# Attention and mixture of experts on one core: widest block first, register reads moved, fills placed anew

## The chip, the cores and the metric

The kernel runs on one core of a Trainium2 chip. The metric is the time of one execution on the device in microseconds (us). Beside timed runs there is one execution under the hardware profiler, with a trace of every engine: TensorE (PE, and PEld for its loads of weights), VectorE (DVE), ScalarE (ACT), GpSimd (POOL) and SyncE (SP). A `q` behind an engine's name (PEldq, ACTq) marks what its sequencer does by itself: branches, register loads, waits.

## The reference

Eight batches of eight heads with 576 positions of 64 numbers pass an attention whose softmaxes stand on q (along the head) and on k (along the sequence). Its output is the input x of a mixture of eight experts: each of 4,608 tokens goes to the expert with the largest logit.

```
q_s = softmax(q, axis=-1);  k_s = softmax(k, axis=2)
kv = einsum('bhsd,bhse->bhde', k_s, v)
x = einsum('bhsd,bhde->bhse', q_s, kv), rearranged to (4608, 512)
logits = x @ w_gate;  expert = argmax(logits);  gate = softmax(logits)[expert]
y = gate * (relu(x @ w1[expert]) @ w2[expert])      # 512 -> 1024 -> 512
```

## The kernel before, in words

There are two parts. The first, `attention_moe`, does the attention of the eight batches, the routing, and the beginning of the first expert. It has no loops at run time: each piece of work is a step with a name (`KM2`, `KV`, `G0`), a batch and a number, and `Plan.emit` puts the steps into an order by planned costs and due times (`COST`, `WHEN`). Rows of x go to a buffer `xs` in memory, sorted by expert.

The table `FILL` names steps ahead of which `fill(n)` puts n matmuls of a 128x128 tile of ones (128x384, L227), whose results nobody reads; `KM2.1.0.18` means 18 of them ahead of step 0 of `KM2` of batch 1. They keep TensorE at work where it would wait. Steps that matter here: `KM2` transposes the maxima of k (kmT, L384) and `KM4` spreads them (mb, L393); `KV` is the product of k and v (L427); `G0` transposes its result (kvT, L452); `TR` and `MM` transpose q and make x (L538, L550); `IT` transposes the first expert's rows.

The second part, `experts`, runs on each engine a loop of its own over steps (`walk`, L1012 to L1016), tied together by semaphores. A step is up to 384 rows of one expert. A table `tab`, written at run time, gives each step's kind (KD, 0 to 12; 12 is 384 rows, 11 is 352, 10 is 320, 9 is 288, 3 to 8 is 256, below 3 a tiny one), its place, and whether it is the last before a new expert's weights (LW). An engine reads it with `x.get`, a register load (L1009).

On TensorE (`pe`) a step is layer 1, eight blocks f of 12 matmuls each (L1033), one copy of the code for each width, and layer 2, up to three times 24 matmuls (L1049), or `half` with 16 (L1091). The loop is preceded by `first(1)` and `first(2)`, layer 2 of rows done in the first part (L1131). On ScalarE (`act`) a step is eight relus (`relus`, L1194), the cast of the next rows of x (`evac`, L1178), that of new W1 (L1231) where weights change, and the output's scaling (`yout`, L1163). In the step after a change of weights, casts of W2 (L1187) stand between the relus. VectorE computes the low parts (HL, L1281), turns the next rows of x (L1260) and subtracts their high parts (XL, L1266). SP loads rows of x and, ahead of their use, the weights (`wload`, L1420 and L1424).

Layer 1 waits for XL at its first matmul, and from f = 5 on for HL of f - 5, whose buffer it takes. Layer 2 waits for HL of each f.

```
            kind = x.get(KD, j, 0, 12)
            fresh = x.get(LW, j, 0, 1)
            turn = x.get(LW, j + 1, 0, 1)
```

These three lines open ScalarE's step; a fourth read, of the next kind, stands behind the relus.

Of the kernel before, what the change touches and what calls it, by code (L numbers as in the profile page):

```python
# [16 lines left out]
P = 128  # L17
# [25 lines left out]
            T4=135.561, T5=67.264, T6=-338.231, T7=192.024, T8=-120.773, T9=1000.0, PD=179.626, SW=73.996)  # L43
WINDOW = 0.0
FILL = """
KM2.0.0.17 KM4.0.0.1 KM2.1.0.18 KM4.1.0.4 KV.0.0.1 KV.0.1.1 KM2.2.0.13 G2.0.0.1 KV.1.1.1 KV.1.2.1 KM2.3.0.4 G0.1.0.7
KM4.3.0.1 TR.1.2.1 KV.2.2.1 R5.0.0.2 MM.1.4.4 KV.3.2.1 G0.3.0.9 TR.3.2.1 G2.3.0.2 KV.4.0.1 KV.4.1.1 KV.4.2.1 KM2.5.0.16
KV.4.3.2 R5.2.0.1 MM.3.0.1 MM.3.1.2 MM.3.2.2 MM.3.3.2 TR.3.4.2 G2.4.0.2 KV.5.2.1 G2.5.0.2 MM.5.0.4 MM.5.1.4 TR.5.4.1
KM4.7.0.14 KV.6.0.1 KV.6.1.1 KV.6.2.1 G0.6.0.5 TR.6.2.2 IT.4.1.1 IT.4.2.4 MM.7.0.1 MM.7.4.2 KV.7.0.1 KV.7.1.1 KV.7.2.2
"""  # L50
KD, ROW, LW, EO, LIVE = range(5)
PE, DVE, ACTE, POOL, SP = "pe", "dve", "act", "pool", "sp"
# [919 lines left out]
def experts(nc, tc, g):  # L972
# [6 lines left out]
    H2, Q = P // 2, P // 4  # L979
# [39 lines left out]
    def pe():  # L1019
        x = Eng(nc.tensor, "pe")  # L1020
        e = nc.tensor
# [3 lines left out]
        def layer1(w):  # L1025
            for f in range(NF):
                if f % 2 == 0:
                    e.wait_ge(sW1[f // 2], it)
                ph = g.PH[f][:, :w]
                n = 0  # L1030
                for wt, xt in ((W1H, g.XH), (W1H, g.XL), (W1L, g.XH)):
                    for c in range(NC):
                        m = e.matmul(ph, wt[:, c, f * P:(f + 1) * P], xt[:, c, :w], start=(n == 0), stop=(n == 3 * NC - 1))  # L1033
                        if n == 0 and f == 0:
                            m.wait_op(sXL, it, GE)
                        if n == 0 and f >= 5:
                            m.wait_op(sHL[PREV[f]], it, GE)
                        n += 1
                m.then_inc(sPH[f], 1)
# [19 lines left out]
        def tiny1():  # L1059
            for h in range(2):  # L1060
                e.wait_ge(sW1[2 * h], it)
                e.wait_ge(sW1[2 * h + 1], it)
                n = 0
                for c in range(NC):
                    for wt in (W1H, W1L):
                        m = e.matmul(g.PH[h], g.XH[:, c, :P], wt[:, c, h * DM:(h + 1) * DM], start=(n == 0), stop=(n == 2 * NC - 1))
                        if n == 0 and h == 0:
                            m.wait_op(sXL, it, GE)
                        n += 1
                m.then_inc(sPH[h], 1)  # L1070
            ones(4)
            for h in range(2):
                if h:
                    ones(3)
                for f in range(4 * h, 4 * h + 4):
                    m = e.matmul(TP[h][:, f - 4 * h, :], HS[:, f * P:(f + 1) * P], g.pair, start=True, stop=True)
                    if f == 4 * h:
                        m.wait_op(sHH[h], it, GE)
                m.then_inc(sPH[2 + h], 1)
            for f in range(4, NF):  # L1080
                e.sem_inc(sPH[f], 1)
# [18 lines left out]

        def body(j):
            kind = x.get(KD, j, 0, 12)
            with e.If(kind < 9):
                with e.If(kind < 3):
                    tiny1()
                with e.If(kind > 2):
                    layer1(2 * P)
            with e.If(kind > 8):
                with e.If(kind < 12):
                    with e.If(kind < 11):  # L1110
                        with e.If(kind < 10):
                            layer1(9 * Q)
                        with e.If(kind > 9):
                            layer1(10 * Q)
                    with e.If(kind > 10):
                        layer1(11 * Q)
                with e.If(kind > 11):
                    layer1(3 * P)
            for u in range(3):
                with e.If(kind > 4 * u + 2):  # L1120
                    layer2(u)
                with e.If(kind < 4 * u + 3):
                    with e.If(kind > 4 * u):
                        half(u)
            x.add("it", 1)
# [26 lines left out]
    def act():  # L1152
        x = Eng(nc.scalar, "act")
        e = nc.scalar
        it, m1, m2 = x.reg("it", 1), x.reg("m1", 16), x.reg("m2", 16)
        cu = [x.reg(f"c{u}", 1) for u in range(3)]
        ou = [x.reg(f"o{u}", 16) for u in range(3)]

        def yout(u, again=True):
            if again:  # L1160
                e.wait_ge(sO[u], ou[u])
                x.add(f"o{u}", 16)
            m = e.activation(g.YT[u], g.PY[u], AF.Copy, scale=g.GA[:, u:u + 1]).wait_op(sPY[u], cu[u], GE)  # L1163
            m.then_inc(sYT[u], 1)
            x.add(f"c{u}", 1)

        def yhalf(u):
            e.wait_ge(sO[u], ou[u])
            x.add(f"o{u}", 16)
            for i, cols in enumerate(HALVES):  # L1170
                m = e.activation(g.YT[u][:H2, cols], g.PY[u][H2:, cols], AF.Copy, scale=g.GA[:H2, u:u + 1])
                if i == 0:
                    m.wait_op(sPY[u], cu[u], GE)
                m.then_inc(sYH, 1)
            x.add(f"c{u}", 1)

        def evac(to=g.XH, src=g.XR):
            e.activation(to, src, AF.Copy).wait_op(sT, it, GE).then_inc(sXH, 1)  # L1178

        def gates():  # L1180
            e.wait_ge(sGS, it)
            for u in range(3):
                e.wait_ge(sYT[u], cu[u])
            e.activation(g.GA, g.GS[:, :, 0], AF.Copy).then_inc(sGA, 1)

        def w2_hi(f):
            m = e.activation(W2H[:, f, :], g.RAW2[:, f, :], AF.Copy)  # L1187
            if f == 0:
                m.wait_op(sR2, m2, GE)
            m.then_inc(sH2[f], 1)  # L1190

        def relus(split):
            for f in range(NF):
                e.activation(g.HH[:, f, :], g.PH[f][:, :W], AF.Relu).wait_op(sPH[f], it, GE).then_inc(sHH[f], 1)  # L1194
                if f == 0:
                    gates()
                if split:
                    w2_hi(f)

        def tiny(split):  # L1200
            w2 = (lambda *fs: [w2_hi(f) for f in fs]) if split else (lambda *fs: None)
            w2(0)
            e.activation(HS[:, :DM], g.PH[0], AF.Copy).wait_op(sPH[0], it, GE).then_inc(sHH[0], 1)
            w2(1)
            gates()
            w2(2)
            for h in range(2):
                e.activation(g.HH[:, 4 * h:4 * h + 4, :H2], TP[h], AF.Relu).wait_op(sPH[2 + h], it, GE).then_inc(sHH[2 + h], 1)
                w2(3 + h)
            w2(5, 6, 7)  # L1210
            for f in range(4, NF):
                e.sem_inc(sHH[f], 1)

        def body(j):
            kind = x.get(KD, j, 0, 12)
            fresh = x.get(LW, j, 0, 1)
            turn = x.get(LW, j + 1, 0, 1)
            for run in (tiny, relus):
                with e.If(kind > 2 if run is relus else kind < 3):
                    with e.If(fresh > 0):  # L1220
                        run(True)
                        x.add("m2", 16)
                    with e.If(fresh < 1):
                        run(False)
            x.add("it", 1)
            with e.If(x.get(KD, j + 1, 0, 12) > 0):
                evac()
            with e.If(turn > 0):
                for q in range(NQ):
                    sl = slice(2 * q * P, 2 * (q + 1) * P)  # L1230
                    m = e.activation(W1H[:, :, sl], g.RAW1[:, :, sl], AF.Copy)  # L1231
                    if q == 0:
                        m.wait_op(sR1, m1, GE)
                    m.then_inc(sH1[q], 1)
                x.add("m1", 16)
            for u in range(3):
                with e.If(kind > 4 * u + 2):
                    yout(u)
                with e.If(kind < 4 * u + 3):
                    with e.If(kind > 4 * u):  # L1240
                        yhalf(u)

        for u in range(3):
            e.sem_inc(sYT[u], 1)
        yout(0, again=False)
        yout(1, again=False)
        evac(g.XH.rearrange("p c (u t) -> p u c t", t=P), g.PT)
        yout(2, again=False)
        x.walk(body)
        for u in range(3):  # L1250
            e.sem_inc(sSp2, 1).wait_op(sO[u], ou[u], GE)
# [233 lines left out]
```

## Time and profile before

| | us |
|---|---|
| median of 3 runs (lowest, highest) | 605.06 (604.38, 607.2) |
| the profiled execution, its own time | 608.49 |
| its span, from the first to the last instruction | 606.7 |

| engine | busy us | share of the span |
|---|---|---|
| PE | 575.0 | 95% |
| PEld | 501.4 | 83% |
| DVE | 323.3 | 53% |
| ACT | 237.0 | 39% |
| POOL | 130.9 | 22% |

The attention stage lasts to about 191 us, the loop of experts begins at about 204 us and has 14 steps. Busy shares are averages over stages with different limits, so they are read by stretch. In the chain of waits, "issue" is time in which the engine waited for nothing that the profile shows as an instruction's work. [...]

### The profile page before, as it was taken

What the parts mean: (1) busy time and instruction counts of PE and PEld (TensorE: products, weight loads), DVE (VectorE), ACT (ScalarE), POOL (GpSimd) and SP (SyncE); (2) the same over time, 40 slices, a digit from 0 to 9 for tenths busy, and PEclk for the clock granted to TensorE, in tenths of its full rate; (3) what the DMA queues carried; (4) which work ended last, traced back from release to release, by engine and by line L of the source; (5) the groups of instructions that cost most, each with busy time, mean ns of one, the idle gap of its engine ahead of it and who ended that gap; (6) DMA issues with size and microseconds to landing.
All of it is one profiled execution on the core that took longest, in us unless ns stands there. A gap on an engine that the chain in (4) does not pass through costs nothing.

```text
span 606.7 us, 12049 instructions
## 1 busy us (share of the span) xinstructions
PE 575.0 (95%) x3858; PEld 501.4 (83%) x3859; DVE 323.3 (53%) x695; ACT 237.0 (39%) x492; POOL 130.9 (22%) x210
## 2 busy tenths in 40 slices
PE   7899999997999499999999999999999999999995
PEld 4677867776887398989989898989989898998983
DVE  6789989995890132252705041426552672566444
ACT  2566537663530112252412121325442542454344
POOL 3122556676250100101010101010101101010110
PEclk9999999999899889999999999999999999999998
DMA  9999998984553923016160302030634147053200
GB/s 262 294 268 242 307 303 227 274 252 173 193 202 118 334 36 70 36 29 213 59 184 0 87 17 70 17 87 6 208 133 104 52 156 226 9 193 143 67 17 22
DMA packets 85313, 86.26 MB, mean 142 GB/s; under 512 B 21024, under 2 KB 70688, under 8 KB 84641
## 3 DMA queue, kind: packets, MB, share of 16 engines
q1 hardware_dynamic: 79280, 66.82, 40.5%
q0 software_dynamic: 6000, 19.03, 8.6%
q8 instruction: 19, 0.31, 0.2%
q14 instruction: 14, 0.11, 0.1%
HBM read 63.88 MB, written 22.74 MB: 143 GB/s over the span
## 4 chain that ended last, share of the span: by engine, by line
PE 81%; DVE 7%; issue 4%; DMA 2%; ACT 2%; SPq 1%; POOL 1%; another core or an unknown queue 0%; DVEq 0%; POOLq 0%; ACTq 0%
PE py L1049 30%; PE pt L1033 23%; PE ph L1033 8%; PE xp L550 3%; PE kv L427 3%; DMA kt<-in_k 2%; PE ph L755 2%; PE py L1131 2%; PE qT L538 1%; PE py L1091 1%; PE kg L461 1%; PE xp L227 1%; DVE kp L375 1%; PE py L769 1%; DVE kt L409 1%
## 5 line engine op out<-in xcount | busy, mean ns | idle before, releaser
L1049 PE MATMUL py<-w2h,hid 128*128 128x512 f32 x528 | 164.8, 389 | 0.0
L1281 DVE SCALAR_TENSOR_TENSOR hid<-pt,hid 128x384 fp32r<-128x384 f32 x78 | 42.8, 557 | 186.9 <-ACT hid L1194 179.2
L1049 PEld LDWEIGHTS py<-w2h,hid 128*128 128x128 f32 x528 | 99.1, 188 | 20.1
L1368 POOL DMA_INDIRECT out<-yt,ix x39 | 42.5, 1089 | 316.4 <-ACT yt L1163 301.7
L1049 PE MATMUL py<-w2l,hid 128*128 128x512 f32 x264 | 102.7, 389 | 0.0
L1194 ACT ACTIVATE hid<-pt 128x384 fp32r<-128x384 f32 x78 | 38.3, 491 | 99.0 <-PE pt L1033 81.5
L1163 ACT ACTIVATE yt<-py,ga 128x512 f32<-128x512 f32 x36 | 24.7, 687 | 131.6 <-PE py L1049 117.9
L1033 PE MATMUL pt<-xh,w1h 128*128 128x384 f32 (+4 forms) x312 | 60.5, 316 | 8.2 <-issue 8.2
L1033 PE MATMUL pt<-xh,w1l 128*128 128x384 f32 (+4 forms) x312 | 59.9, 314 | 0.0
L1033 PE MATMUL pt<-xl,w1h 128*128 128x384 f32 (+4 forms) x312 | 59.9, 314 | 0.0
L1033 PEld LDWEIGHTS pt<-xh,w1h 128*128 128x128 f32 x312 | 51.2, 192 | 9.6 <-issue 8.6
L1049 PEld LDWEIGHTS py<-w2l,hid 128*128 128x128 f32 x264 | 49.6, 188 | 9.9
L1033 PEld LDWEIGHTS pt<-xl,w1h 128*128 128x128 f32 x312 | 50.3, 191 | 0.0
L1033 PEld LDWEIGHTS pt<-xh,w1l 128*128 128x128 f32 x312 | 50.3, 191 | 0.0
L663 POOL DMA_INDIRECT xs<-xr,posi x36 | 36.9, 1024 | 47.3 <-DVE lh L565 25.1
L1260 DVE STREAM_TRANSPOSE xrow<-xt 128x1536 f32<-128x1536 f32 x13 | 38.6, 2973 | 0.0
L550 PE MATMUL xp<-kx,qTs 128*128 128x146 f32 x256 | 37.3, 292 | 1.3 <-ACT kx L445 0.7
L550 PEld LDWEIGHTS xp<-kx,qTs 128*128 128x128 f32 x256 | 33.3, 190 | 3.9 <-issue 1.5
L543 ACT ACTIVATE qTs<-qT 128x512 f32<-128x512 f32 x36 | 21.1, 596 | 29.8 <-PE xp L550 15.8
L227 PEld LDWEIGHTS <-ones 128*128 128x128 bf16 x212 | 21.1, 102 | 14.1 <-issue 3.1
L497 POOL TENSOR_TENSOR qs<-qt,qm 128x1024 f32<-128x1024 f32 (+1 forms) x16 | 23.8, 1512 | 41.2 <-DVE qm L492 34.1
L1272 DVE TENSOR_TENSOR w2l<-raw,w2h 128x512 fp32r<-128x512 f32 x40 | 27.2, 689 | 6.9 <-ACT w2h L1187 6.7
(246 smaller groups left out, 883.3 us busy)
## 6 DMA issues: line engine op xcount, KB each, us to landing
raw<-in_moe_w SPq DMA_DIRECT2D x10, 2048.0 KB, 9.3
vt<-in_v SPq DMA_DIRECT2D x16, 512.0 KB
qt<-in_q SPq DMA_DIRECT2D x8, 1024.0 KB
kt<-in_k SPq DMA_DIRECT2D x7, 1024.0 KB
xt<-xs SPq DMA_DIRECT2D x32, 192.0 KB
xs<-zr SPq DMA_DIRECT2D x11, 260.0 KB
xt<-in_moe_w SPq DMA_DIRECT2D x8, 256.0 KB
raw<-in_moe_w SPq DMA_DIRECT2D x4, 512.0 KB
```

The source lines that it names most:

```text
L227: nc.tensor.matmul(hot.t if to is None else to, ones16, ones16[:, None, :].to_broadcast([P, HOT // P, P]), start=True, stop=True)
L497: nc.gpsimd.tensor_tensor(o.qs[:, j0:j1].rearrange("p j h d -> p h j d"), o.qt[:, :, j0:j1, :], o.qm[:, :, j0:j1, None].to_broadcast([P, H ...
L550: nc.tensor.matmul(xv[:, c, :KW], o.qT[i][:, c, :], kx[:, c, :], start=True, stop=True)
L663: s = nc.gpsimd.indirect_dma_start(out=xs, out_offset=bass.IndirectOffsetOnAxis(ap=n.pi[:, t - t0:t - t0 + 1], axis=0), in_=xr[:, t, :], i ...
L1033: m = e.matmul(ph, wt[:, c, f * P:(f + 1) * P], xt[:, c, :w], start=(n == 0), stop=(n == 3 * NC - 1))
L1049: m = e.matmul(g.PY[u], ht[:, f, u * P:(u + 1) * P], wt[:, f, :], start=(n == 0), stop=(n == 3 * NF - 1))
L1163: m = e.activation(g.YT[u], g.PY[u], AF.Copy, scale=g.GA[:, u:u + 1]).wait_op(sPY[u], cu[u], GE)
L1194: e.activation(g.HH[:, f, :], g.PH[f][:, :W], AF.Relu).wait_op(sPH[f], it, GE).then_inc(sHH[f], 1)
L1260: e.transpose(g.XR.rearrange("p c (k j) -> p k c j", j=32), xblocks(g.XT).rearrange("p k (l c) -> p k c l", c=NC)).wait_op(sX, ld, GE).the ...
L1272: m = e.tensor_tensor(W2L[:, f, :], g.RAW2[:, f, :], W2H[:, f, :].bitcast(F32), op=ALU.subtract).wait_op(sH2[f], n2, GE)
L1281: e.scalar_tensor_tensor(g.HL[:, f, :], g.PH[f][:, :W], 0.0, g.HH[:, f, :].bitcast(F32), op0=ALU.max, op1=ALU.subtract).wait_op(sHH[f], it ...
L1368: e.indirect_dma_start(out=g.out, out_offset=bass.IndirectOffsetOnAxis(ap=g.IX[:, u:u + 1], axis=0), in_=g.YT[u], in_offset=None, bounds_c ...
```

## The change

There are three edits.

1. In `pe`'s step the choice among the copies of layer 1 is turned around: the comparison for kind 12 and its block, 384 wide, stand first, then those of kinds 11, 10 and 9, then the 256 wide one and the tiny one.
2. In `act` the kind and LW of a step are no longer read at its start. The next step's two values are read behind the relus (before, one of them was) and kept in registers `kd` and `lw`, which are set once before the loop.
3. `FILL` is written anew: 196 fills in place of 172, in other places.

```diff
 FILL = """
-KM2.0.0.17 KM4.0.0.1 KM2.1.0.18 KM4.1.0.4 KV.0.0.1 KV.0.1.1 KM2.2.0.13 G2.0.0.1 KV.1.1.1 KV.1.2.1 KM2.3.0.4 G0.1.0.7
-KM4.3.0.1 TR.1.2.1 KV.2.2.1 R5.0.0.2 MM.1.4.4 KV.3.2.1 G0.3.0.9 TR.3.2.1 G2.3.0.2 KV.4.0.1 KV.4.1.1 KV.4.2.1 KM2.5.0.16
-KV.4.3.2 R5.2.0.1 MM.3.0.1 MM.3.1.2 MM.3.2.2 MM.3.3.2 TR.3.4.2 G2.4.0.2 KV.5.2.1 G2.5.0.2 MM.5.0.4 MM.5.1.4 TR.5.4.1
-KM4.7.0.14 KV.6.0.1 KV.6.1.1 KV.6.2.1 G0.6.0.5 TR.6.2.2 IT.4.1.1 IT.4.2.4 MM.7.0.1 MM.7.4.2 KV.7.0.1 KV.7.1.1 KV.7.2.2
+KM2.0.0.17 KM4.0.0.4 KM2.1.0.26 KM4.1.0.10 KM2.2.0.18 KM4.2.0.1 KM2.3.0.2 G0.1.0.5 R5.0.0.2 MM.1.4.5 G0.3.0.9 G2.3.0.3
+KM2.5.0.12 KV.4.3.1 MM.3.1.2 MM.3.3.3 TR.3.4.5 G2.4.0.2 G2.5.0.2 MM.5.0.4 MM.5.1.4 TR.5.4.1 KM4.7.0.14 G0.6.0.5
+TR.6.2.2 G2.6.0.2 KV.7.2.1 G0.7.0.4 IT.4.1.2 IT.4.2.2 MM.7.4.2 KV.0.1.1 KV.0.0.1 G2.0.0.1 KV.1.0.1 KV.1.1.3 G2.1.0.1
+KM4.3.0.1 TR.1.2.1 KV.2.2.1 KV.3.1.1 TR.3.2.1 KV.4.0.1 KV.4.1.2 R5.2.0.1 KV.5.2.1 KV.5.1.1 KV.6.0.1 KV.6.1.1 KV.6.2.1
+KV.7.1.1 G2.7.0.1
 """
...
             kind = x.get(KD, j, 0, 12)
-            with e.If(kind < 9):
-                with e.If(kind < 3):
-                    tiny1()
-                with e.If(kind > 2):
-                    layer1(2 * P)
-            with e.If(kind > 8):
-                with e.If(kind < 12):
+            with e.If(kind > 11):
+                layer1(3 * P)
+            with e.If(kind < 12):
+                with e.If(kind > 8):
+                    with e.If(kind > 10):
+                        layer1(11 * Q)
                     with e.If(kind < 11):
+                        with e.If(kind > 9):
+                            layer1(10 * Q)
                         with e.If(kind < 10):
                             layer1(9 * Q)
-                        with e.If(kind > 9):
-                            layer1(10 * Q)
-                    with e.If(kind > 10):
-                        layer1(11 * Q)
-                with e.If(kind > 11):
-                    layer1(3 * P)
+                with e.If(kind < 9):
+                    with e.If(kind > 2):
+                        layer1(2 * P)
+                    with e.If(kind < 3):
+                        tiny1()
...
         def body(j):
-            kind = x.get(KD, j, 0, 12)
-            fresh = x.get(LW, j, 0, 1)
-            turn = x.get(LW, j + 1, 0, 1)
+            kind = e.snap(kd, min_val=0, max_val=12)
+            fresh = e.snap(lw, min_val=0, max_val=1)
...
             x.add("it", 1)
-            with e.If(x.get(KD, j + 1, 0, 12) > 0):
+            more = x.get(KD, j + 1, 0, 12)
+            turn = x.get(LW, j + 1, 0, 1)
+            with e.If(more > 0):
                 evac()
...
+            e.reg_mov(kd, more)
+            e.reg_mov(lw, turn)
...
+        kd, lw = x.reg("kd", x.get(KD, 0, 0, 12)), x.reg("lw", x.get(LW, 0, 0, 1))
         x.walk(body)
```

How the instructions stand, in the listing of the built programs. Lines of the changed kernel are higher by one and more, as its code is longer. First TensorE at the head of its loop, before; `pt` and `ph` are layer 1's outputs, `xh` and `xl` the rows of x, `w1h` and `w1l` the weights:

```order
L1016 ISA
L1009 TENSOR_LOAD tab
L1009 ISA x2
L1103 COMPARE_AND_BRANCH
L1104 COMPARE_AND_BRANCH
L1066 MATMUL pt<-w1h_61,xh 128x512
...
L1115 UNCONDITIONAL_BRANCH
L1117 COMPARE_AND_BRANCH
L1033 MATMUL pt<-xh,w1h_61 128x384 x4
...
L1117 UNCONDITIONAL_BRANCH
L1120 COMPARE_AND_BRANCH
L1006 REGISTER_ALU
```

and the same head now:

```order
L1017 ISA
L1010 TENSOR_LOAD tab
L1010 ISA x2
L1104 COMPARE_AND_BRANCH
L1034 MATMUL pt<-xh,w1h_61 128x384 x4
L1034 MATMUL pt<-xl,w1h_61 128x384 x4
L1034 MATMUL pt<-xh,w1l_62 128x384 x4
...
L1104 UNCONDITIONAL_BRANCH
L1106 COMPARE_AND_BRANCH
L1107 COMPARE_AND_BRANCH
```

The block of 384 moved from behind all others (before it stand the tiny one with 38 matmuls and four of 96) to the place right behind the first comparison; from its end a step of kind 12 now jumps over the others to layer 2, which before followed it directly.

ScalarE from the end of the relus to the cast of x (`xh`), before and now:

```order
L1223 UNCONDITIONAL_BRANCH
L1006 ISA
L1009 TENSOR_LOAD tab
L1009 ISA x2
L1226 COMPARE_AND_BRANCH
L1178 ACTIVATE xh<-xrow 128x1536
```

```order
L1223 UNCONDITIONAL_BRANCH
L1007 ISA
L1010 TENSOR_LOAD tab
L1010 ISA x3
L1010 TENSOR_LOAD tab
L1010 ISA x2
L1228 COMPARE_AND_BRANCH
L1179 ACTIVATE xh<-xrow 128x1536
```

One more register load stands ahead of the cast of x; the three at the head of the loop are gone, and two stand ahead of the loop.

TensorE in the attention stage at the end of batch 6's x (`xp`) and the beginning of kvT of batch 7, before and now:

```order
L427 MATMUL kv<-vt_93,kt 64x65 x20
L538 MATMUL qT<-ident,qsr 128x128 x4
L538 MATMUL qT<-ident,qs 128x128 x4
L550 MATMUL xp<-kx_98,qTs 128x146 x8
L452 MATMUL kvT<-ident,kx_99 128x128 x4
L741 MATMUL pt_2187<-ident,xt 128x128 x4
```

```order
L539 MATMUL qT<-ident,qsr 128x128 x4
L539 MATMUL qT<-ident,qs 128x128 x4
L551 MATMUL xp<-kx_98,qTs 128x146 x8
L228 LDWEIGHTS ones_109
L228 MATMUL rk<-ones_109 128x384
...
L453 MATMUL kvT<-ident,kx_99 128x128 x4
L742 MATMUL pt_2212<-ident,xt 128x128 x4
```

Four fills (`G0.7.0.4`) now stand between the two. Apart from fills and the choice of block, TensorE's order is unchanged, and the orders of VectorE, GpSimd and SP are unchanged altogether.

## Rows read from the trace of the kernel before

**Rows 1.** Stretches of the span: from:to, length, then busy us and instructions by engine.

```profile
core 0: us, PE busy (x) PEld busy (x) DVE busy (x) ACT busy (x) POOL busy (x), PEclk, DMA share, GB/s
...
204.00:231.36 27.36, 19.19 (x98) 19.15 (x98) 6.64 (x8) 4.23 (x9) 1.17 (x2) 0.81 0.45 122
231.36:594.00 362.64, 362.64 (x2007) 329.01 (x2007) 154.34 (x196) 128.96 (x217) 40.77 (x47) 1.00 0.31 92
```

**Rows 2.** The chain of waits from the loop's head on: start us, us, what.

```profile
204.07 8.17 issue
212.24 8.71 PE pt L1033 x36
...
231.36 16.33 PE py L1049 x72
247.69 6.24 PE pt L1033 x36
```

**Rows 3.** Timeline around the loop's head, VectorE: start us, us, engine, line, operation.

```profile
202.17 1.76 DVE L1266 TENSOR_TENSOR xl<-pt,xh 128x1536 fp32r<-128x1536 f32 x1 [16.38 <-ACT xh L1178]
...
221.99 2.94 DVE L1260 STREAM_TRANSPOSE xrow<-xt 128x1536 f32<-128x1536 f32 x1
```

**Rows 4.** TensorE's branches, one line each: duration ns min/median/max, first and last start us.

```profile
L1103 PEldq COMPARE_BRANCH  x14: 71/212/2947, 201.0 to 586.3; - x14
...
L1109 PEldq COMPARE_BRANCH  x9: 72/204/7737, 204.1 to 537.1; - x9
```

**Rows 5.** DMA queues in 204 to 212, 217 to 231, 242 to 606 us.

```profile
q8 instruction: 2, 0.03, 2.9%
...
DMA  0000000000000001000000000000000000000000
...
q8 instruction: 1, 0.02, 0.4%
...
q1 hardware_dynamic: 23488, 24.07, 23.2%
q0 software_dynamic: 2808, 8.42, 6.3%
issues: line engine op xcount, KB each, median us to landing
```

**Rows 6.** Short stretches, columns as in rows 1: the granted clock (PEclk).

```profile
152.00:156.00 4.00, 3.76 (x20) 3.57 (x20) 3.19 (x9) 2.66 (x6) 0.00 (x0) 0.57 0.00 0
...
206.00:208.00 2.00, 0.00 (x0) 0.00 (x0) 0.00 (x0) 0.00 (x0) 0.66 (x1) 0.71 1.08 394
...
212.00:217.00 5.00, 4.76 (x15) 4.79 (x16) 0.02 (x1) 0.55 (x2) 0.19 (x1) 0.50 0.77 123
```

**Rows 7.** TensorE's branch ahead of layer 2, as in rows 4.

```profile
L1120 PEldq COMPARE_BRANCH  x42: 65/70/213, 228.1 to 599.6; - x42
```

**Rows 8.** Branches of ScalarE and VectorE ahead of the first relu; VectorE's low parts.

```profile
L1223 ACTq COMPARE_BRANCH  x14: 40/40/50, 207.3 to 595.4; - x14
...
L1319 DVEq COMPARE_BRANCH  x14: 50/50/63, 206.9 to 598.4; - x14
...
L1281 DVE SCALAR_TENSOR_TENSOR hid<-pt,hid x78: 539/558/575, 217.0 to 578.1; 128x384 fp32r<-128x384 f32 x78
```

**Rows 9.** ScalarE: its register loads, and the first cast of W2 in the last step.

```profile
L1009 ACTq TENSOR_LOAD <-tab x56: 272/278/318, 205.1 to 595.8; - x56
...
591.42 0.63 ACT L1187 ACTIVATE w2h<-raw 128x512 fp32r<-128x512 f32 x1 [2.24 <-issue]
```

**Rows 10.** The attention stage: two pieces of the chain, two waits of TensorE (timeline).

```profile
30.79 9.22 DMA kt<-in_k
...
83.61 2.71 PE xp L227 x16
...
17.00 0.63 PE L384 MATMUL kmT<-ident,km 128*128 128x128 f32 x4 [1.27 <-DVE km L379]
...
152.24 1.11 PE L452 MATMUL kvT<-ident,kx 128*128 128x128 f32 x4 [3.69 <-ACT qTs L543]
```

## The prediction

> **What bounds the kernel now.** I read the stretch view first [rows 1]: from 231.36 to 594.00 us TensorE is busy 362.64 of 362.64 us at full clock, so there only fewer or shorter matmuls can help, and the change alters none. What is left is the attention stage, the passage into the loop of experts, and the tail. In 204.00 to 231.36 TensorE is busy 19.19 of 27.36 us at a mean clock of 0.81, the worst stretch.
>
> The chain of waits names the loss [rows 2]: 204.07 to 212.24, 8.17 us of "issue", just ahead of the first matmul of the first layer 1, and that layer's first 36 matmuls take 8.71 us where the same 36 of the next step take 6.24. The wait is not for data. XL is written at 202.17 + 1.76 = 203.93 [rows 3], before the pause begins.
>
> The sequencer's branches say what it is [rows 4]. The branch at L1103 takes 2.95 us at its longest and starts first at 201.0; the one at L1109 takes 7.74 us at its longest and starts first at 204.1, so it ends at 211.9, the moment before TensorE starts. Their medians are 0.21 and 0.20 us. In the same 8 us the instruction queue q8 moves two packets of 16 KB while the queues are full of the experts' weights, and in 217 to 231 one more; from 242 to 606 it moves none, though every width of layer 1 still runs for its first time but the widest [rows 5]. So a branch costs microseconds where its target was never fetched, and 0.2 us once it was. [...]
>
> **What the change does, part by part.**
>
> *Order of blocks on TensorE.* Before, the first step (kind 12) jumps from L1103 over the tiny block and the 256 wide one, then from L1109 over three blocks, into the 384 wide one, and falls into layer 2. Now the 384 wide block follows the first comparison and is fallen into; the far jump, over four blocks and the tiny one, comes behind it.
> Removed: the idle 212.24 - 204.07 = 8.17 us. TensorE would start the layer when its last matmul of `first(2)` ends at 204.07, since XL is there at 203.93 and the sequencer was at L1103 at 201.0. Without a pause I expect no fall of the clock, which came behind one: 8.71 - 6.24 = 2.47 us. Together 10.64.
> Added: one long branch behind the block, since layer 2's code is then the part never fetched. Its lower end is 0.2 us (a known target), its upper end 7.74. I take L1103's 2.95, because the queues then carry almost nothing: in 217 to 231 their busy digits are 0 but for one fetch [rows 5], and the weights do not start earlier, as SP issues them before the loop. From the branch's end to the first matmul went 212.24 - 211.88 = 0.36. Of this the sequencer's lead is hidden: it reached L1120 at 228.1 while layer 2 began on TensorE at 231.36 [rows 2, 7], a lead of 3.26 us. New idle 2.95 + 0.36 - 3.26 = 0.05; with the upper end 7.74 + 0.36 - 3.26 = 4.84. In later steps all code is there, and branches hide behind a TensorE with no idle: 0.
>
> *What is late next.* A block f of layer 1 is 12 matmuls of 6.24/36 us, 2.08 us, the layer 16.64. It would run 204.07 to 220.71. ScalarE's branches were done at 207.3 and VectorE's at 206.9 [rows 8], while the first block ends at 206.15; so the first relu is up to 1.1 us late, but TensorE first wants its result at f = 5, at 214.5. VectorE turns the next rows of x ahead of f = 3 (2.94 us, now at 221.99 [rows 3]) and must wait for them to land. The queues are empty from 217 on [rows 5], so at worst it turns them from 217 to 220 and writes HL[3] to HL[7] at 0.56 each [rows 8], by 222.8. Layer 2 wants HL[3] at 220.7 + 3 x 0.68 = 222.7 and HL[7] at 225.5 (16.33/24 = 0.68 per f [rows 2]). No wait: 0.
>
> *ScalarE's registers.* A step began with three register loads of 0.28 us each [rows 9], with their other instructions about 0.6 each; now one more load stands behind the relus and none at the start. In steps that TensorE fills this is hidden: 0. The one visible place is the last step, where ScalarE sits 2.24 us on "issue" before its first cast of W2 [rows 9]. There I take 0 too: the casts of f = 0 to 2 come earlier, but the relus behind them wait for TensorE's turn of the tiny rows, and VectorE's chain of W2L behind these ends as before. Bounds: 0 to 1.85 (three loads) gained; nothing lost, as the extra 0.6 us ahead of the x cast stands under 16.33 us of layer 2.
>
> *Fills.* 172 become 196. One costs 2.71/16 = 0.169 us [rows 10]. Up to 40 us there are 24 more (4.1 us), where TensorE waits anyway (1.27 us at 17.00, for one) and the chain runs through a load of K of 9.22 us up to 40.01 [rows 10]. After that 25 places change with a sum of zero; of these the one on the chain is KM2.5, 16 to 12: -0.68. Four new ones stand before kvT of batch 7, in a pause of 3.69 us [rows 10] after which the clock was at half until 155.7 (0.57 on average in 152 to 156 [rows 6]). They leave a pause of 3.0 us; the clock fell 2.8 us into the other one, so I count no gain. The fills together: 0, between +2.8 (4.1 less 1.27, nothing else hidden) and -2.4 (0.68, and half of 3.4 us at half clock).
>
> **Sum.** -8.17 - 2.47 + 0.05 + 0 = -10.6 us. The profiled execution's 608.49 would become 597.9. The median of the runs is 605.06, 3.4 below it, and gives 594.5.
>
> **A rule against it.** Once fetched, code stays: L1109 has a median of 0.20 us over its nine uses [rows 4], and q8 is silent after 242 [rows 5]. If it did not stay, the jump behind the block would wait in each of the 13 later steps too, up to 13 x 4.84 = 63 us more; before, the jumps of those steps would have waited as well and did not, so this gets no chance beyond rival 3. [...]
>
> **Rivals.**
> 1. The miss only moves. The branch behind the block costs its upper price, as if the queues were full: 4.84 us idle, 605.06 - 10.64 + 4.84 = 599.3, and 601.7 if the clock falls again (2.47). For it: the only branch that is known to have waited for its own fetch took 7.74. Against: the queues were full then, and are empty now. Chance 0.14.
> 2. The timed runs hold less of this stall than the profiled one, up to the 3.4 us by which they are faster: 598. For it: the stall hangs on other transfers, and the three runs spread over 2.8 us. Chance 0.08.
> 3. Slower: the other blocks' code is no longer fetched on the way, since the first step no longer passes them, and each of the four narrower widths (320, 256, 352, 288) waits for it at its first use. At 4.84 us each that is 19.4 - 10.6 = +8.8, 613.8; it decides from 10.6/4 = 2.6 us each. Against: fetches also run ahead of the code, one is seen in 217 to 231 while no branch waits, and TensorE's lead hides 3.26. Chance 0.04.
> 4. The change doesn't do what it says: the 24 added fills push the loop's code along, the end of the 384 wide block is not there when the loop is entered, and the wait moves into the block instead of away: 603 to 605. Chance 0.06.
>
> **How the numbers follow.** The forecast has 0.68. Its range runs from 605.06 - 10.64 - 2.4 = 592.0 to 600.5, which holds rival 2, and rival 1 without a second fall of the clock. About 0.5%, 3.0 us, is what a measurement of this kernel can tell from no change. Faster: forecast, rival 2 and 0.10 of rival 1, 0.86. Within it: 0.04 of rival 1 and rival 4, 0.10. Slower: 0.04.
>
> **What would show it.** Right: in the new chain no "issue" of microseconds between `first(2)` and layer 1; the first 36 matmuls of layer 1 in about 6.24 us; clock 1.00 from 204 to 217; one branch of 2 to 4 us behind the 384 wide block, with under 1 us of idle before layer 2; TensorE without idle from there to about 583. The attention stage ends within 2 us of 204. Wrong: a branch of over 5 us there, several long branches at the first narrower steps, or a wait of VectorE for x that reaches TensorE.

## The result, and the profile after

| kernel, first comparison | median us (lowest, highest), runs | ratio to before, 95% interval |
|---|---|---|
| before | 606.12 (604.38, 607.2), 4 | |
| changed | 596.41 (595.15, 598.32), 4 | 0.9845 [0.9806, 0.9884] |

The changed kernel is faster by 9.7 us, 1.6%. The forecast was 594.5 us, 10.6 less than the median shown then. The profiled execution took 595.15 us with a span of 593.4, against 608.49 and 606.7: 13.3 us less, more than the medians say. The chain of waits of the changed kernel, from the end of the attention stage on (start us, us, what):

```profile
185.23 0.83 issue
...
199.03 6.42 PE pt L1034 x36
205.46 4.16 PE ph L1034 x24
209.62 6.24 PE pt L1034 x36
215.86 0.76 issue
216.62 16.60 PE py L1050 x72
```

Before, 8.17 us of issue stood ahead of the first layer 1, and its first 36 matmuls took 8.71 us [rows 2]. Now there is none, they take 6.42, and a small piece of issue, 0.76 us, has come up behind the block. The stretch view shows the granted clock there (PEclk, a share of full speed), and its short stretches answer to [rows 6]:

```profile
core 0: us, PE busy (x) PEld busy (x) DVE busy (x) ACT busy (x) POOL busy (x), PEclk, DMA share, GB/s
204.00:216.00 12.00, 11.86 (x69) 11.54 (x67) 5.81 (x7) 2.56 (x6) 0.19 (x1) 1.00 0.48 112
152.00:156.00 4.00, 4.00 (x44) 3.67 (x44) 3.26 (x19) 1.40 (x4) 0.00 (x0) 1.00 0.91 249
...
212.00:217.00 5.00, 4.24 (x25) 3.91 (x24) 4.33 (x6) 1.21 (x3) 0.00 (x0) 1.00 0.03 7
```

TensorE's branches, one line each, as in [rows 4]: the one behind the 384 wide block, and one that the first narrower step meets:

```profile
L1106 PEldq COMPARE_BRANCH  x14: 76/76/3607, 212.6 to 573.4; - x14
...
L1115 PEldq COMPARE_BRANCH  x9: 73/73/2964, 376.8 to 573.8; - x9
```

The long branch stands where it was expected, at 212.6, with 3.61 us. A second one, of 2.96 us at 376.8, was not expected. The chain around it, and the instruction queue in 360 to 395 us, where before it moved nothing after 242 [rows 5]:

```profile
373.91 5.28 PE pt L1034 x36
379.19 0.97 issue
380.16 11.16 PE py L1050 x48
...
q8 instruction: 4, 0.07, 0.8%
```

The same step before:

```profile
388.38 5.28 PE pt L1033 x36
393.66 10.91 PE py L1049 x48
```

The spans add up as follows. The loop begins at 199.03 instead of 204.07: -5.04. From there to layer 2 it takes 216.62 - 199.03 = 17.59 us instead of 231.36 - 204.07 = 27.29: -9.70. From layer 2 to the end it takes 593.4 - 216.62 = 376.78 instead of 606.7 - 231.36 = 375.34: +1.44. The sum is -13.30. The middle term is the one that the change was forecast by. The third is made of three parts: the wait of 0.97 us at the first step of 320 rows, 0.27 for the first layer 2 (16.60 instead of 16.33), and 0.2 behind them. The first had to be explained by experiments.

### The profile page after: what moved, and what is told of

Read it like the earlier page. It is cut to its first block, busy times and chain, and to the rows that moved or that the text cites. A ratio compares the mean times of both kernels' runs of the same rounds, so it can differ in the third digit from the quotient of the medians.

```text
span 593.4 us, 12007 instructions
## 1 busy us (share of the span) xinstructions
PE 574.5 (97%) x3882; PEld 500.0 (84%) x3883; DVE 324.0 (55%) x695; ACT 237.4 (40%) x492; POOL 132.8 (22%) x210
## 4 chain that ended last, share of the span: by engine, by line
PE 85%; DVE 8%; issue 2%; ACT 2%; DMA 2%; SPq 0%; DVEq 0%; POOL 0%; POOLq 0%; ACTq 0%
PE py L1050 30%; PE pt L1034 24%; PE ph L1034 8%; PE kv L428 4%; PE xp L551 3%; PE ph L756 2%; PE py L1132 2%; PE qT L539 2%; DMA kt<-in_k 2%; PE py L1092 1%; DVE qm L493 1%; DVE xr L568 1%; DVE kt L410 1%; PE py L770 1%; ACT kx L446 1%
## 5 line engine op out<-in xcount | busy, mean ns | idle before, releaser
L228 PEld LDWEIGHTS <-ones 128*128 128x128 bf16 x236 | 23.2, 101 | 15.2 <-issue 2.7
L544 ACT ACTIVATE qTs<-qT 128x512 f32<-128x512 f32 x36 | 21.1, 595 | 25.4 <-PE xp L551 15.5
L1271 DVE TENSOR_TENSOR xl<-xrow,xh 128x1536 fp32r<-128x1536 f32 x12 | 21.1, 1758 | 18.6 <-ACT xh L1179 18.6
```

The source lines that it names most:

```text
L228: nc.tensor.matmul(hot.t if to is None else to, ones16, ones16[:, None, :].to_broadcast([P, HOT // P, P]), start=True, stop=True)
```

## Experiments: the three edits apart

Three kernels are the kernel before with one edit each: e_blocks has edit 1, e_act edit 2, e_fill edit 3, each word for word as in the diff above. after_again is the changed kernel. The four ran on one chip with one set of runs of the kernel before.

e_blocks:

> The kernel before with the new order of the widths' blocks alone. Theory (the order of the blocks takes the stall ahead of the first layer 1 away, fills and registers are worth nothing): 8.2 us of idle and 2.3 us of slow clock go, 0.8 us of idle comes back behind the 384 wide block and 1.0 us at the first narrower width, so 8 to 9.5 us faster than before; in the profile no issue of microseconds between first(2) and layer 1, and one branch of 3 to 4 us behind the block. Rival (the new fills did half of it, by taking away the pause ahead of kvT of batch 7 that the profile of before shows at 148.6 to 152.2 us, and the half clock behind it): 4 to 5 us faster only, with that pause of 3 to 4 us and the half clock still in the profile.

e_fill:

> The kernel before with the new fills alone. Theory: within 1 us of before; the stall of 7 to 9 us ahead of the first layer 1 is still there. Rival (the fills take away the pause ahead of kvT of batch 7): 4 to 5 us faster, no pause over 1 us there, no half clock in 140 to 160 us, and the loop of experts entered some 5 us earlier.

e_act:

> The kernel before with the loads of ScalarE's registers moved behind the relus, alone. Theory: within 0.5 us of before; in the last step ScalarE's issue ahead of its first cast of W2 falls from 2.2 us to under 1, and the end does not move. Rival (the casts of the last step are on the path to the end): up to 1.9 us faster, all of it after the last matmul of the last full step. Its fills are the old ones, so if the pause ahead of kvT of batch 7 belongs to them it is seen here again at 3 to 4 us; if it was one execution's own, it may be missing.

after_again:

> The changed kernel again, beside its parts on the same chip. Theory: 9 to 10 us faster than before, equal to the blocks alone within 1 us; the attention stage ends at the same time as in the profiles of the parts. Rival (blocks and fills each give about half): the blocks alone and the fills alone, added, give its 9 to 10 us.

| kernel | median us, runs | ratio to before (604.21 us, 18 runs) | profiled span |
|---|---|---|---|
| e_blocks | 596.16, 4 | 0.9864 [0.9835, 0.9893] | 595.0 |
| e_fill | 601.14, 7 | 0.9939 [0.9915, 0.9962] | 599.7 |
| e_act | 604.61, 12 | 1.0001 [0.9984, 1.0019] | 603.3 |
| after_again | 595.81, 4 | 0.9868 [0.9839, 0.9897] | 593.3 |

**The order of the blocks** alone gives 8.05 of the 8.4 us. (For the whole change beside its parts 9 to 10 us had been expected; 8.4 is less.) Its chain shows the same as the changed kernel's, with 0.89 us behind the block:

```profile
200.51 6.42 PE pt L1033 x36
206.94 4.16 PE ph L1033 x24
211.10 6.24 PE pt L1033 x36
217.34 0.89 issue
218.23 16.57 PE py L1049 x72
```

**The registers** are worth nothing in the time. In the last step ScalarE's idle ahead of the casts of W2 falls from the 2.24 us of [rows 9] to 0.5, and nothing follows from it. The group of the casts in the last step of e_act (busy us, mean ns, idle before it):

```profile
L1187 ACT ACTIVATE w2h<-raw 128x512 fp32r<-128x512 f32 x8 | 4.7, 623 | 0.5 <-issue 0.5
```

**The pause ahead of kvT** of batch 7 [rows 10] is not the fills' matter. With the old fills it is missing in e_act and in e_blocks. Their stretches of 10 us around it (columns as above; e_act's two lines, then e_blocks'):

```profile
140.00:150.00 10.00, 9.58 (x129) 7.80 (x128) 7.37 (x28) 5.87 (x20) 7.61 (x13) 1.00 0.44 154
150.00:160.00 10.00, 9.91 (x88) 8.48 (x86) 8.45 (x34) 5.50 (x12) 3.40 (x8) 1.00 0.78 287
```

```profile
140.00:150.00 10.00, 9.58 (x129) 7.80 (x128) 7.43 (x28) 5.69 (x21) 7.31 (x13) 1.00 0.40 135
150.00:160.00 10.00, 10.00 (x89) 8.80 (x89) 8.40 (x34) 5.50 (x12) 3.69 (x8) 1.00 0.77 280
```

TensorE idles 0.51 and 0.42 us in these 20 us, at full clock. With the new fills a pause of like length came up once, 3.1 us in e_lay2pad below, there ahead of the matmul behind kvT (L742). So pauses of this size came with either set of fills, in 2 of the 11 profiles taken, and that of before had one. What held ScalarE up, for which TensorE waited in both, is not shown. The pause is most of the -5.04, and would account for a profiled pair that differs by more than the medians.

**The fills** alone give 3.1 us, which neither theory had forecast. The loop's head in the two kernels with the old order, e_act with the old fills and then e_fill with the new ones:

```profile
200.18 9.12 issue
209.30 8.34 PE pt L1033 x36
```

```profile
198.99 5.80 issue
204.79 9.18 PE pt L1034 x36
```

Three things differ. The loop begins 1.2 us earlier, the stall is 3.3 us shorter, and the 36 matmuls behind it take 0.84 us more. The 1.2 us come from 80 to 98 us, in batches 4 and 5, where fewer fills stand ahead of the first step of KM2 of batch 5 (16 to 12); at the prediction's 0.169 us a fill these are worth 0.68, and the rest is not traced to single fills. VectorE's first product of K's halves (`kp`) runs from 80.6 to 98.4 in e_act and from 80.4 to 97.0 in e_fill (first and last start, four instructions each):

```profile
L375 DVE TENSOR_TENSOR kp<-kt x4: 670/682/3983, 80.6 to 98.4; 128x512 f32<-128x512 f32 x4
```

```profile
L376 DVE TENSOR_TENSOR kp<-kt x4: 670/680/3849, 80.4 to 97.0; 128x512 f32<-128x512 f32 x4
```

The stretch from one step of the maxima of K (km, L379, now L380) near 86 us to the next near 101 takes 15.5 to 16.0 us in the four profiles with the old fills and 14.4 to 14.8 in the seven with the new ones. Yet the loop's head itself moves by as much from profile to profile: e_lay2in and e_lay2all below, with the new fills, begin it at 200.41 and 200.44 us.

The shorter stall shows in the branches. In e_act the first comparison and the second take 3.75 and 7.89 us at their longest; in e_fill the same two take 0.37 and 7.97:

```profile
L1103 PEldq COMPARE_BRANCH  x14: 71/212/3747, 197.1 to 583.0; - x14
...
L1109 PEldq COMPARE_BRANCH  x9: 72/204/7887, 201.1 to 533.8; - x9
```

```profile
L1104 PEldq COMPARE_BRANCH  x14: 71/212/370, 196.0 to 579.3; - x14
...
L1110 PEldq COMPARE_BRANCH  x9: 72/204/7974, 196.5 to 530.1; - x9
```

One of the two long branches is gone, 0.37 us instead of 3.75, though no code of the loop was changed. The new theory was that 24 fills more, 48 instructions, shift the loop against the pieces in which code is fetched (the instruction queue's packets are of 16 KB: 19 of them with 0.31 MB in the whole profile of before). The instruction queue fits it: in e_act its packet starts only in 197.1 to 200.9, while L1103 waits, and in e_fill already in 185 to 195.9, before L1103 (there L1104) begins at 196.0 (one line each):

```profile
q8 instruction: 1, 0.02, 1.5%
```

```profile
q8 instruction: 1, 0.02, 0.6%
```

The next kernel tests it.

## Experiments: the length of the code ahead, and the load of the queues

e_pad is the kernel before with 24 more fills in one place, far from the loop; e_load is the changed kernel with one load moved:

```diff
 e_pad (kernel before), FILL:
-KM2.0.0.17 KM4.0.0.1 KM2.1.0.18
+KM2.0.0.41 KM4.0.0.1 KM2.1.0.18
 e_load (changed kernel), SP ahead of its loop:
-            wload(x.get(EO, 1, 0, E - 1), False)
+            a = e.dma_start(g.RAW1, w1v[bass.ds(x.get(EO, 1, 0, E - 1) * P, P)])
+            a.then_inc(sR1, 16)
 and in SP's step, behind rows(j + 1):
+            with e.If(e.snap(it, min_val=1, max_val=MAXS) < 2):
+                with e.If(x.get(LIVE, 1, 0, 1) > 0):
+                    b = e.dma_start(g.RAW2, ...)
+                    b.wait_op(sPH[5], 1, GE)
+                    b.then_inc(sR2, 16)
```

e_pad:

> The kernel before with 24 more fills, all ahead of the first use of K in batch 0, so that TensorE's program has as many instructions ahead of the loop as with the new fills, and the order of the blocks is the old one. Theory (the new fills help the old order by their number: the last 16 KB of code ahead of the loop is entered some 10 us earlier, the piece behind it has landed when L1103 jumps into it, and one of the two waits is gone): L1103 at 0.3 us or less instead of 2.9 to 3.7, the idle ahead of the first layer 1 5 to 6.5 us instead of 8 to 9, 2 to 3.5 us faster than before, less up to 2 us for fills that delay batch 0. Rival (the new fills help by their places in the attention stage): L1103 still at 3 to 4 us, idle 8 to 9 us, 0 to 3 us slower than before.

It took 602.83 us against 604.47 of before on the same chip, ratio 0.9969 [0.9951, 0.9988]. The chain, and the first comparison:

```profile
201.60 4.98 issue
206.58 8.79 PE pt L1033 x36
```

```profile
L1103 PEldq COMPARE_BRANCH  x14: 71/212/373, 198.6 to 580.7; - x14
```

L1103 is at 0.37 us, the stall at 4.98 instead of 9.12, and the loop begins 1.4 us later than in e_act, as these fills delay batch 0. The bounds of the theory were 0.3 and 5 us, so both are just outside them, and the way is as forecast. That the last 16 KB of code ahead of the loop is entered some 10 us earlier was the author's estimate; no run shows what code a packet holds. What takes the wait at L1103 away is thus the number of instructions ahead of the loop, not their places; the earlier start of the loop in e_fill is not part of this. In the new order, where the first step has only one far jump, the number has no such wait to remove: the changed kernel and e_blocks differ by 0.35 us in the medians, and the parts, 8.05 and 3.1, don't add up to the whole.

e_load:

> The changed kernel, with the 2 MB of the second expert's W2, which are wanted only after 260 us, loaded once block 5 of the first layer 1 is done instead of at 191 us: the queues are then full when TensorE jumps from the 384 wide block to layer 2. Theory (the price of a jump to code never fetched hangs on the load of the queues): the branch of L1106 lasts 5.5 to 8 us instead of 3.3 to 3.6, TensorE idles 2.5 to 5 us ahead of layer 2 instead of 0.5 to 0.8, and the time is 2 to 4 us above the changed kernel's. Rival (the price is that of the jump and its place; the 7.7 to 8.0 us of the old order come of two pieces of code fetched in a row): 3.2 to 4 us and under 1 us of idle, the time as the changed kernel's.

It took 601.5 us, ratio 0.9942 [0.9918, 0.9965] to the same runs of before. Its chain, its branch, the queues in 212 to 220 and the stretches around the pause:

```profile
216.25 3.59 issue
219.84 18.18 PE py L1050 x72
```

```profile
L1106 PEldq COMPARE_BRANCH  x14: 76/76/6440, 213.0 to 578.3; - x14
```

```profile
q1 hardware_dynamic: 1033, 2.08, 73.3%
```

```profile
216.25:219.84 3.59, 0.00 (x1) 0.03 (x1) 1.24 (x2) 1.97 (x2) 0.00 (x0) 1.00 0.92 346
219.84:223.20 3.36, 3.35 (x8) 2.68 (x9) 1.15 (x2) 0.00 (x0) 0.00 (x0) 0.50 0.04 10
```

The same branch to the same code takes 6.44 us instead of 3.34 (after_again) to 3.61, because weights move meanwhile: q1 carries 2.08 MB in 212 to 220, in which the changed kernel's queues carry two packets of the instruction queue, 0.03 MB, and nothing else. A clock of 0.50 for 3.4 us follows the pause. The theory holds for this jump: its price at its first use hangs on the load of the queues. The instruction queue tells where the time goes: its packet starts 0.95 us after the branch in the changed kernel (213.55) and 3.95 us after it here (216.95); from there to the branch's end 2.7 and 2.5 us pass. The time came out 5.7 us above after_again's 595.81, more than the 2 to 4 expected. The two ran on different chips, but the profiles show 4.7 of it between the end of layer 1 and that of layer 2: 3.59 instead of 0.49 us of idle, and 18.18 instead of 16.57 us for layer 2. The second part is the clock, which the expectation had left out.

## Experiments: hiding the remaining waits

Three variants of the changed kernel put a copy of the first 128 rows' layer 2 behind the 384 wide block (e_lay2in), behind each wide block (e_lay2all), or as the first with 32 matmuls more that no step reaches (e_lay2pad).

```diff
 e_lay2in:
             with e.If(kind > 11):
                 layer1(3 * P)
+                layer2(0)
...
+                with e.If(kind > 2):
+                    layer2(0)
+                with e.If(kind < 3):
+                    with e.If(kind > 0):
+                        half(0)
-            for u in range(3):
+            for u in (1, 2):
 e_lay2pad, in addition, inside kind < 3:
+                    with e.If(kind > 5):
+                        ones(32)
```

e_lay2in:

> The changed kernel with the first 128 rows' layer 2 written once more directly behind the 384 wide block, so that the far jump comes behind it. Theory (the jump's wait of 3.3 to 3.7 us is hidden as far as TensorE's sequencer runs ahead, and in layer 2, where one matmul takes 0.23 us instead of 0.17, it runs ahead by more time, some 4.3 us): no idle over 0.1 us there, the wait of 1.0 us at the first narrower width stays; 0.5 to 0.8 us below the changed kernel. Rival (the lead is the same in time, or the longer code costs a fetch more): the idle of 0.5 to 0.9 us comes behind the first 24 matmuls of layer 2 and nothing is gained.

e_lay2all:

> As the kernel with layer 2 behind the 384 wide block, but behind each of the five wide blocks. Theory: both waits are hidden, 1.3 to 1.8 us below the changed kernel, no idle of TensorE on issue over 0.1 us from 199 us to the last step. Rival (208 more instructions need a piece of code more, and each width has its own copy to fetch): one or more new waits of 1 us at first uses, and no gain.

e_lay2pad:

> The kernel with the first 128 rows' layer 2 once more behind the 384 wide block, and 32 matmuls that no step reaches in the branch of the narrow widths, so that the code behind the far jump lies some 30 instructions further on. Theory (that kernel's idle of 2.4 us came of where the jump lands, shortly ahead of the end of a piece of 16 KB, so that a second piece was waited for): the branch behind the first layer 2 still lasts 3.3 to 3.7 us, it is hidden by the sequencer's lead of 4.2 us, there is no idle of TensorE on issue between 199 and 360 us; 2.4 us faster than that kernel. Rival (the copy of layer 2 lengthens the code, and a second piece is always waited for behind it): an idle of 2 to 3 us is there again, and the time is that kernel's.

| kernel | median us, runs | ratio to before on its chip |
|---|---|---|
| e_lay2in | 598.63, 6 | 0.9897 [0.9865, 0.9928] |
| e_lay2all | 597.0, 6 | 0.9859 [0.9826, 0.9893] |
| e_lay2pad | 601.11, 6 (before there 613.37) | 0.9797 [0.9757, 0.9838] |

The chain of e_lay2in, and its branch:

```profile
217.23 5.44 PE py L1050 x24
222.68 2.42 issue
225.09 11.07 PE py L1050 x48
```

```profile
L1107 PEldq COMPARE_BRANCH  x14: 73/73/3377, 218.5 to 576.4; - x14
```

The branch runs from 218.5 us for 3.38 us and ends at 221.9, before the 24 matmuls do, at 222.68: the lead in layer 2 is 4.2 us, as expected, and covers it. Yet 2.42 us are lost behind it; the rival's idle is there, larger than it said. In e_lay2pad, whose code behind the jump lies a little further on, the branch lasts 3.75 us and layer 2 runs through:

```profile
216.26 6.24 PE pt L1034 x36
222.50 16.49 PE py L1050 x72
```

So the copy hides the jump, and the 2.42 us came of where the jump lands. That a second piece of code was waited for fits the instruction queue of e_lay2in, which starts one packet in the branch (at 219.4) and a second behind it (at 222.5), 2.6 us before TensorE goes on. In e_lay2pad a second packet starts too (at 228.6), and TensorE does not wait for it. Which code a packet holds is not shown. The 2.4 us in time that were expected of e_lay2pad can't be read from the medians: it ran on another chip, where the kernel before took 613.37 us instead of 604.47.

e_lay2all runs through its first layer 2 as well (217.28, 16.33 us), but its first narrower step waits longer, 2.91 us, with half a clock behind it:

```profile
385.05:387.96 2.91, 0.00 (x1) 0.03 (x1) 0.00 (x0) 0.69 (x1) 0.99 (x1) 1.00 0.37 99
387.96:391.30 3.34, 3.34 (x8) 2.66 (x9) 0.00 (x0) 0.00 (x0) 0.00 (x0) 0.50 0.99 234
```

Its rival was right. None of the three ran beside the changed kernel, and none is shown to beat it. What is left to hide is 0.76 and 0.97 us; e_lay2pad hides the first and waits 1.35 instead of 0.97 for the second, a net of some 0.4 us that the medians can't tell.

## Why the prediction was right, and where it was off

**Removed idle.** Right. In the pair that ran side by side without the pause (e_act, whose time is that of before, and after_again) the stretch from the loop's head to layer 2 falls from 228.04 - 200.18 = 27.86 to 216.64 - 199.32 = 17.32 us, by 10.54; the forecast for it was 10.64 - 0.05. So close a hit is partly luck: the stall was larger than forecast (9.12 us), the clock gave back less (8.34 - 6.42 = 1.92), and new idle of 0.49 us came up. In the first pair the same stretch fell by 9.70.

**Clock.** Right: before, it was 0.50 in 212 to 217 [rows 6]; now it is 1.00 throughout. In the first pair the first 36 matmuls give back 2.29 of 2.47 us.

**The new branch.** Right in place and kind, too low in price. The step "I take L1103's 2.95" gave 0.05 us of idle; the branch took 3.61, 3.34 and 3.74 in three profiles, and 3.61 + 0.36 - 3.26 = 0.71 is what the trace shows, 0.76. That empty queues make the price of this jump lower is confirmed by e_load (6.44 us with q1 busy 73.3% of 212 to 220). But L1103 was no measure of it: in its 201.0 to 203.95 us the weights' queue q1 was busy 82.5% of the time. That its 2.95 comes near the 3.34 to 3.74 measured with empty queues is luck.

**Later steps: 0.** This step failed, by 0.97 us. "In later steps all code is there" held in the kernel before, whose instruction queue is silent after 242 us; in the changed kernel the first narrower width, 320, waits. Rival 3 had the place but not the branch: those into the block of 320 take 0.21 us at most (362.3 to 363.4), and the one that waits leads out of it (L1115, below). Its four waits of 4.84 were one of 0.97, as 352, 288 and 256 pass without any such idle in the chain.

**What is late next: nothing.** Right. VectorE turned the next x at 211.0 instead of 217 to 220 and TensorE waited for none of its results.

**ScalarE's registers: 0.** Right, by e_act.

**Fills: 0.** Off within its bounds. In e_act and e_fill they bring the loop's head forward by 1.2 us, where the text had named 0.68 for KM2.5 and then counted nothing; in the medians of e_blocks and after_again it is 0.35, too little to tell from nothing. The bound had no term for the shift of the code, which is the larger effect in the old order and gives nothing in the new one. Rival 4 had it with the wrong sign.

**The sum.** Too much was forecast by 0.71 and 0.97 us, and up to 1.2 us of the fills was left out. Against the medians of before, 605.06 at the time and 604.21 to 606.12 since (613.37 on e_lay2pad's chip), the chance for rival 2 was not needed: the stall is in e_act's profile at 9.12 us. The 608.49 of the profiled execution fits the pause ahead of kvT, not the stall, which was shorter there (8.17).

## What to carry to other kernels

Where an engine enters a loop for the first time, lay the code that its first step takes in a row (8.05 us here), and put the first far jump where the queues are empty and the engine's queue is full of work: here its branch of 3.61 us left 0.76 us of idle, and with the queues loaded one of 6.44 us left 3.59. The branches' longest durations in the trace beside their medians (3.61 and 0.08 us at L1106) tell where to look for such waits. Before a gain is put down to a fill or a delay, count the instructions: a change of 48 ahead of a loop took L1103 from 3.75 to 0.37 us. And check a pause of one profiled execution in a second one before costing anything by it.

## What was not expected of the hardware

Code that had run before was waited for again. L1115, at the first step of 320 rows, jumps to the first comparison of layer 2, which had run in each of the five steps before it, and lasted 2.96 us (2.97 in e_blocks) while the instruction queue, silent from 226 to 365 us, moved packets again. In the old order no such wait is in the chain. The four steps of 384 rows in this silence jump out and back each time without one: L1106, which jumps to the same code in them, takes 0.22 us at most in 226 to 365. What was fetched at the first narrower step, and why, is not shown.

Pauses of like length were followed by different clocks. Behind 2.42 us without work in e_lay2in TensorE went on at full clock, behind 2.91 us in e_lay2all the granted clock was 0.50 for 3.3 us (shown above):

```profile
222.68:225.09 2.41, 0.00 (x0) 0.00 (x0) 0.00 (x0) 0.69 (x1) 0.81 (x1) 1.00 0.15 36
225.09:228.50 3.41, 3.40 (x15) 2.82 (x15) 0.00 (x0) 0.00 (x0) 0.18 (x1) 1.00 1.09 261
```
